# Balancing the sort matrices with row products written transposed

## The chip, the cores and the metric

The kernel runs on one core of a Trainium2 chip. Its engines work side by side, each on its own queue of instructions: TensorE (PE) multiplies matrices, VectorE (DVE) and ScalarE (ACT) do elementwise work and reductions, GpSimd (POOL) does small elementwise work and issues most loads, SyncE (SP) issues transfers. They wait for each other by semaphores. The metric is the device time of one execution in microseconds (us).

## The reference

There are 32 sort matrices of 8 x 8 (4 batches of 8 heads). Each is balanced in five rounds; then its rows mix the eight blocks of keys and values, block attention follows, and a feed-forward network with two first layers takes the larger of both. What the change touches is the first loop:

```
P = sort_net                                   # (4, 8, 8, 8)
for _ in range(5):
    P = P - np.max(P, axis=-1, keepdims=True)
    P = np.exp(P)
    P = P / (np.sum(P, axis=-1, keepdims=True) + 1e-09)
    P = P / (np.sum(P, axis=-2, keepdims=True) + 1e-09)
k_sorted = np.einsum('bhij,bhjcd->bhicd', P, k_b)
v_sorted = np.einsum('bhij,bhjcd->bhicd', P, v_b)
...
```

The rest is softmax(q k_sorted^T / 8) v_sorted for each of the eight blocks of 96 tokens, and then max(x w1, x w2) w_out on 3072 tokens of width 512. Sequence 768, head width 64, inner width 1024.

## The kernel before, in words

The kernel is one list of steps, written out by hand as short tokens (the string `plan`), which the function `token` turns into instructions one after the other. Each engine runs its own instructions in that order. So the list alone sets what stands in front of what on an engine, and nothing is reordered later. The start of the list, which holds the five rounds of balancing (S0 to S4), the masks (m0 to m3), the first turns of v (tv) and the block diagonal matrices made of the result (D0, B0), reads:

```
lw1 lw2 I1 lk0.0 lk0.1 lk0.2 lq0.0 lq0.1 lq0.2 S0 m0 S1 m1 S2 m2 tv0.18A S3 tv18.36A lq0.3
J1 S4 m3 tv36.56A tv56.80A D0 g1 tv80.96D g2 g3 a2.0.1 B0 k0.1A k0.0A k0.2A b0.0A q0.0D
```

**Balancing** (`sinkhorn`, lines 269 to 288). The tile p_sb holds one matrix on each of 32 partitions, 64 floats in the order i, j (row, column). A round has one ScalarE instruction, the exponential (L270), and six on VectorE: the row sums (L276), their reciprocals (L277), the product of each row with its own (L278), the column sums (L281), which read p_sb with i and j exchanged, that is 8 floats or 32 bytes apart from number to number, their reciprocals (L282), and the product of each column with its own (L283). The last product of the fifth round goes to p_bf in bf16. The subtraction of the maximum is left out, since it cancels. In the fourth and fifth round (`it >= 3`) a tile of zeros is set (L88) and TensorE is given filler matmuls (L83, tile fill_ps), which compute nothing that is used.

**Beside it.** TensorE runs fillers from the start. ScalarE copies pieces of v (L250, `turn_v`), reading pairs of bf16 numbers 128 bytes apart and writing in order; VectorE copies one such piece as 4-byte words (L255). VectorE also makes the masks (L294 to L311) behind the rounds, and POOL the selections (L211, L218, L226) and more masks (L1068) once its first loads are issued.

**Behind it.** `block_diagonals_first` multiplies p_bf on TensorE (L361, L368), VectorE makes the block diagonal matrix for the keys (L376), and TensorE mixes the keys with it (L489, tile k_ps). ScalarE copies that out of PSUM (L109, tile kT), and scores (L584), exponentials (L599), values (L612), their division by the sums (L629) and the feed-forward layers (L805, L961) follow. Queries are turned in PSUM and copied out to the tile qT, by L109 in order for batch 0 and by L466 with pairs of bf16 numbers written 192 bytes apart for batch 1. The masked sums L391 and L342 are two reductions of VectorE that read in order, of 64 and of 320 floats a partition. Batches 1 to 3 have transposes of x by DMA (tile xT).

Of the kernel before, what the change touches and what calls it, by code (L numbers as in the profile page):

```python
# [10 lines left out]
FP32 = mybir.dt.float32  # L11
# [5 lines left out]
def kernel(  # L17
# [16 lines left out]
    nc = tc.nc  # L34
    AF = mybir.ActivationFunctionType
    ALU = mybir.AluOpType
    AX = mybir.AxisListType

    B, H, S, D = q.shape
    NB = sort_net.shape[-1]  # L40
    BLK = S // NB
    G = B * H
# [13 lines left out]
    const = ctx.enter_context(tc.tile_pool(name="const", bufs=1))  # L56
# [10 lines left out]
    def ps_f32(name):  # L67
        return psum.tile([128, 1024], FP32, tag="ps", name=name)
# [9 lines left out]
    def keep_streaming(ps, n, by=None, most=512):  # L78

        w0 = fill[:, 0:128] if by is None else late[by]  # L80
        while n > 0:
            w = min(n, most)
            nc.tensor.matmul(ps[:, 0:w], w0, fill[:, 0:w], start=True, stop=True)  # L83
            n -= w

    def late_zeros(by):
        late[by] = const.tile([128, 128], BF16, tag=f"late{by}", name="late")
        nc.vector.memset(late[by], 0.0)  # L88
# [25 lines left out]
    p_sb = const.tile([G, NB, NB], FP32, tag="p_sb", name="p_sb")  # L114
# [150 lines left out]
    rowsum = const.tile([G, NB], FP32, tag="rowsum", name="rowsum")  # L265
    colsum = const.tile([G, NB], FP32, tag="colsum", name="colsum")
    p_bf = const.tile([G, NB, NB], BF16, tag="p_bf", name="p_bf")

    def sinkhorn(it, meanwhile=None):
        nc.scalar.activation(out=p_sb, in_=p_sb, func=AF.Exp)  # L270
        if meanwhile:
            meanwhile()
        if it >= 3:
            late_zeros(it)
            keep_streaming(ps_f32("fill_ps"), 3072, it)
        nc.vector.reduce_sum(out=rowsum, in_=p_sb, axis=AX.X)  # L276
        nc.vector.reciprocal(out=rowsum, in_=rowsum)  # L277
        nc.vector.tensor_tensor(  # L278
            out=p_sb, in0=p_sb, in1=rowsum.to_broadcast([G, NB, NB]), op=ALU.mult
        )  # L280
        nc.vector.reduce_sum(out=colsum, in_=p_sb.transpose([0, 2, 1]), axis=AX.X)  # L281
        nc.vector.reciprocal(out=colsum, in_=colsum)  # L282
        nc.vector.tensor_tensor(  # L283
            out=p_bf if it == 4 else p_sb,
            in0=p_sb,
            in1=colsum.to_broadcast([G, NB, NB]).transpose([0, 2, 1]),
            op=ALU.mult,
        )

# [791 lines left out]
    def token(text):  # L1081
# [8 lines left out]
        elif kind == "J":  # L1090
            first_selections()
        elif kind == "S":
            sinkhorn(n[0])
        elif kind == "m":
            masks(n[0]) if n[0] < 3 else spread_masks()
# [141 lines left out]
```

## Time and profile before

| | |
|---|---|
| median of the runs shown | 156.07 us (155.84 to 156.44) |
| the profiled execution | 156.11 us |
| its span, first to last instruction | 154.3 us |
| busy: PE, DVE, ACT, POOL | 147.4, 134.7, 102.0, 25.3 us |
| first exponential starts, p_bf is written | 2.49 us, 11.49 to 11.70 us |
| first matmul of the attention (L361) | 11.76 us |
| granted clock of TensorE | 1.00 in the mean |

The profile is a record of one execution. Its chain of waits goes back from the last instruction to what released it, and on to the first; shares and times of that chain tell what set the end. A group has the line of the code, the engine, the operation, the written tile, an arrow, the read tiles, the shape, and how many there were; behind the bar stand busy us and mean ns of one; behind the next bar the idle time ahead of them. Busy shares alone mislead here: PE is busy in the first 12 us, but with fillers.

### The profile page before, as it was taken

Reading aid. Unit: us, or ns where it says so; the run is one execution under the profiler, and the core shown is the slowest. Engines: PE = TensorE matmul, PEld = TensorE weight load, DVE = VectorE, ACT = ScalarE, POOL = GpSimd, SP = SyncE. Lnnn points to the kernel's source line nnn. Section 1 sums busy time; section 2 is a strip of 40 time slices with the busy share of each in tenths; the row PEclk is TensorE's granted clock in tenths of the full one; section 3 lists DMA queues with packets and bytes.
Section 4 is the critical chain, followed back from the end, with each engine's and each line's share of the span. In section 5 each row is a group of like instructions: output and inputs, shape, how many; then the busy total and the mean of one; then the engine's idle time right before and its main releaser. Section 6 shows DMA issues by size and latency. Waiting matters only on the chain.

```text
span 154.3 us, 5157 instructions
## 1 busy us (share of the span) xinstructions
PE 147.4 (96%) x2238; PEld 114.0 (74%) x2238; DVE 134.7 (87%) x287; ACT 102.0 (66%) x134; POOL 25.3 (16%) x53
## 2 busy tenths in 40 slices
PE   6999989999999999999999999989999999999991
PEld 6948867555678788887567998765688978578881
DVE  4888989999999999986999999658899999999731
ACT  3488897268899997879859797888792301463010
POOL 7999541100210400001500000000000000000000
PEclk9999999999999999999999999999999999999999
DMA  3999999999999972998999939996001475500065
GB/s 45 197 207 197 197 204 207 217 215 215 216 215 199 205 155 57 150 133 219 287 205 211 188 62 150 165 195 253 0 4 24 85 116 203 187 6 0 0 224 184
DMA packets 28918, 23.93 MB, mean 155 GB/s; under 512 B 16672, under 2 KB 24608, under 8 KB 28896
## 3 DMA queue, kind: packets, MB, share of 16 engines
q0 software_dynamic: 9280, 13.37, 49.1%
q1 hardware_dynamic: 19200, 9.84, 28.9%
q10 hardware_dynamic: 416, 0.39, 0.8%
q8 instruction: 17, 0.28, 0.7%
q14 instruction: 5, 0.04, 0.1%
HBM read 26.75 MB, written 6.29 MB: 214 GB/s over the span
## 4 chain that ended last, share of the span: by engine, by line
PE 62%; DVE 24%; ACT 4%; DMA 3%; issue 3%; DVEq 0%
PE out_ps L961 32%; PE hb_ps L805 10%; PE hq_ps L805 8%; PE o_ps L612 4%; DVE g L824 4%; DVE x L629 3%; PE k_ps L489 3%; PE s_ps L584 3%; DMA xT<-x 2%; ACT kT L109 2%; DVE w_sb L771 2%; PE v_ps L554 1%; DVE v_dc L255 1%; DVE sums_x L891 1%; DVE w_sb L236 1%
## 5 line engine op out<-in xcount | busy, mean ns | idle before, releaser
L805 PEld LDWEIGHTS <-w_sb 128*128 128x128 bf16 x224 | 21.5, 98 | 14.7 <-issue 0.8
L599 ACT ACTIVATE e<-s_ps 96x768 bf16<-96x768 f32 x32 | 24.1, 807 | 2.2 <-PE s_ps L584 2.0
L629 DVE TENSOR_TENSOR x<-o_ps,rs 96x512 bf16<-96x512 f32 x32 | 22.0, 686 | 1.1
L996 ACT COPY o<-out_ps 128x512 f32<-128x512 f32 (+1 forms) x18 | 8.6, 479 | 21.5 <-PE out_ps L961 21.2
L961 PEld LDWEIGHTS <-g 128*128 128x128 bf16 x192 | 18.2, 98 | 2.4
L805 PE MATMUL hb_ps<-sums_x,w_sb 128*128 128x384 bf16 x96 | 18.2, 327 | 0.0
L961 PEld LDWEIGHTS <-sums_g 128*128 128x128 bf16 x144 | 13.5, 97 | 2.2 <-issue 0.2
L961 PE MATMUL out_ps<-wo_sb,g 128*128 128x256 bf16 x96 | 13.1, 273 | 0.0
L987 DVE TENSOR_TENSOR o<-out_ps,o 128x512 f32<-128x512 f32 (+1 forms) x16 | 8.9, 553 | 4.7 <-PE out_ps L961 4.6
L109 ACT CAST kT<-k_ps 128x1024 bf16<-128x1024 f32 x12 | 11.6, 1020 | 2.0 <-PE k_ps L489 2.0
L805 PE MATMUL hq_ps<-xT,w_sb 128*128 128x384 bf16 x64 | 12.7, 326 | 0.0
L612 PE MATMUL o_ps<-v_sb,e 96*128 96x65 bf16 x256 | 12.4, 194 | 0.0
L612 PEld LDWEIGHTS <-e 96*128 96x128 bf16 x256 | 10.7, 98 | 1.5 <-DVE x L629 0.2
L961 PE MATMUL out_ps<-w2T,sums_x 128*128 128x256 bf16 x72 | 11.8, 273 | 0.0
L584 PE MATMUL s_ps<-qT,kT 64*128 64x96 bf16 x256 | 9.2, 204 | 1.1 <-ACT qT L109 0.7
L111 DVE CAST v_sb<-v_ps 96x1024 bf16<-96x1024 f32 x8 | 9.6, 1214 | 0.2 <-PE v_ps L531 0.2
L961 PEld LDWEIGHTS <-sums_x 128*128 128x128 bf16 x96 | 8.6, 97 | 1.2
L584 PEld LDWEIGHTS <-kT 64*128 64x128 bf16 x256 | 6.4, 94 | 3.5 <-issue 2.6
L826 ACT ACTIVATE g<-g 128x768 bf16<-128x768 bf16 x7 | 5.9, 842 | 4.4 <-DVE g L824 4.4
L83 PE MATMUL fill_ps<-fill 128*128 128x118 bf16 x92 | 7.3, 264 | 1.2 <-DVE fill L74 1.2
L176 POOL DMA_DIRECT2D v_raw<-in_v_dram x11 | 6.5, 597 | 11.2 <-DVE v_dc L255 4.3
L109 ACT CAST v_sb<-v_ps 96x1024 bf16<-96x1024 f32 x8 | 7.8, 1016 | 0.6 <-PE v_ps L554 0.6
(129 smaller groups left out, 304.2 us busy)
## 6 DMA issues: line engine op xcount, KB each, us to landing
out_dram<-o SPq DMA_DIRECT2D x10, 512.0 KB, 2.9
v_raw<-in_v_dram POOLq DMA_DIRECT2D x8, 384.0 KB, 16.2
k_raw<-in_k_dram POOLq DMA_DIRECT2D x3, 768.0 KB, 10.8
w_sb<-in_moe_w_dram POOLq DMA_DIRECT2D x4, 256.0 KB, 7.6
wo_sb<-in_moe_w_out_dram POOLq DMA_DIRECT2D x2, 512.0 KB, 11.2
w_sb<-in_moe_w_dram POOLq DMA_DIRECT2D x2, 512.0 KB, 14.8
v_raw<-in_v_dram POOLq DMA_DIRECT2D x3, 256.0 KB, 4.7
k_raw<-in_k_dram POOLq DMA_DIRECT2D x3, 256.0 KB, 6.4
```

The lines of the kernel that those rows point to most:

```text
L83: nc.tensor.matmul(ps[:, 0:w], w0, fill[:, 0:w], start=True, stop=True)
L109: nc.scalar.copy(out=out_ap, in_=in_ap)
L111: nc.vector.tensor_copy(out=out_ap, in_=in_ap)
L176: nc.gpsimd.dma_start(out=v_raw[r0 : r0 + 64, m * n : (m + 1) * n], in_=v_src[b, :, m * n : (m + 1) * n],)
L584: nc.tensor.matmul(ps[:, h2 * 512 + ii * 128 : h2 * 512 + ii * 128 + BLK], kT[b][rows, (hp * 8 + i) * BLK : (hp * 8 + i) * BLK + 128], rhs ...
L599: nc.scalar.activation(out=e_out, in_=src, func=AF.Exp, scale=scale)
L612: nc.tensor.matmul(ps[:, h2 * 512 + ii * 65 : h2 * 512 + (ii + 1) * 65], e[:, (h2 * 4 + ii) * BLK : (h2 * 4 + ii) * BLK + 128], v_sb[:, m0 ...
L629: nc.vector.tensor_tensor(out=x, in0=ov[:, :, :, 0:D], in1=rs.to_broadcast([BLK, 2, 4, D]), op=ALU.mult,)
L805: nc.tensor.matmul(ps[:, m * 512 : m * 512 + TCH], w[:, k, c : c + 128], x[:, k], start=new and k == 0, stop=k == 1, skip_group_check=True,)
L961: ins = nc.tensor.matmul(self.ps[:, bank * 512 + p * NW : bank * 512 + (p + 1) * NW], left(self.b, lw, k, ti * 128), right(rw, k), start=n ...
L987: ins = nc.vector.tensor_tensor(out=self.part(ch, half), in0=self.by_tile(self.bank(n)), in1=other, op=ALU.add)
L996: ins = nc.scalar.copy(out=out, in_=self.by_tile(self.bank(n)))
```

## The change

A new tile p_t, 32 partitions of 64 floats, holds the matrices in the order j, i. The row product reads p_sb as before and writes p_t, in the order i, j of the instruction, so that each number is written 32 bytes behind the last. The column sums read p_t in order. The column product reads and writes p_t in order, with each column's factor repeated along the inner axis; in the fifth round it reads p_t in order and writes p_bf across, numbers of 2 bytes 16 bytes apart, so that p_bf holds what it held before. From the second round on the exponential reads p_t across, 32 bytes from float to float, and writes p_sb in order; the first round's works in p_sb as before. The list of steps, the number of instructions and their order on every engine are the same.

```diff
+    p_t = const.tile([G, NB, NB], FP32, tag="p_t", name="p_t")
 
     def sinkhorn(it, meanwhile=None):
-        nc.scalar.activation(out=p_sb, in_=p_sb, func=AF.Exp)
+        if it:
+            nc.scalar.activation(out=p_sb, in_=p_t.transpose([0, 2, 1]), func=AF.Exp)
+        else:
+            nc.scalar.activation(out=p_sb, in_=p_sb, func=AF.Exp)
...
         nc.vector.tensor_tensor(
-            out=p_sb, in0=p_sb, in1=rowsum.to_broadcast([G, NB, NB]), op=ALU.mult
-        )
-        nc.vector.reduce_sum(out=colsum, in_=p_sb.transpose([0, 2, 1]), axis=AX.X)
+            out=p_t.transpose([0, 2, 1]),
+            in0=p_sb,
+            in1=rowsum.to_broadcast([G, NB, NB]),
+            op=ALU.mult,
+        )
+        nc.vector.reduce_sum(out=colsum, in_=p_t, axis=AX.X)
         nc.vector.reciprocal(out=colsum, in_=colsum)
         nc.vector.tensor_tensor(
-            out=p_bf if it == 4 else p_sb,
-            in0=p_sb,
-            in1=colsum.to_broadcast([G, NB, NB]).transpose([0, 2, 1]),
+            out=p_bf.transpose([0, 2, 1]) if it == 4 else p_t,
+            in0=p_t,
+            in1=colsum.to_broadcast([G, NB, NB]),
             op=ALU.mult,
         )
```

## The prediction

> **What bounds the kernel now.** I read the page's chain of waits first, then the same chain in order of time, then the instructions that write or read the tile p_sb, then the groups kept apart by shape.
>
> ```profile
> PE 62%; DVE 24%; ACT 4%; DMA 3%; issue 3%; DVEq 0%
> ```
>
> Over the whole span TensorE is the bound, but the change lies in the first 12 us, and there the chain is another. The chain in order of time, with start, length, engine and tile (one iteration, and the handover to the sorting of the keys):
>
> ```profile
> 6.41 0.22 DVE rowsum L276
> 6.65 0.20 DVE rowsum L277
> 6.88 0.22 DVE p_sb L278
> 7.13 0.27 DVE colsum L281
> 7.42 0.20 DVE colsum L282
> 7.65 0.22 DVE p_sb L283
> 7.89 0.26 ACT p_sb L270
> 8.18 0.22 DVE rowsum L276
> ...
> 11.49 0.22 DVE p_bf L283
> 11.76 0.36 PE pe L361 x8
> 12.19 0.23 DVE bd L376
> 12.47 0.71 PE k_ps L489 x32
> 13.20 2.84 ACT kT L109 x3
> ```
>
> Six VectorE instructions and one exponential follow each other with 0.02 to 0.04 us between them, five times, and the end of the last releases the first useful matmul (L361). So every instruction of the balancing is on the path, and a nanosecond added to one of them is added to the start of the attention. The PE work beside it (fill_ps) is filler that computes nothing, so it hides nothing.
>
> The tile's own rows, with the shortest, median and longest time in ns:
>
> ```profile
> L270 ACT ACTIVATE p_sb<-p_sb x5: 255/255/257, 2.5 to 9.8; 32x64 f32<-32x64 f32 x5
> L276 DVE TENSOR_REDUCE rowsum<-p_sb x5: 206/207/207, 2.8 to 10.1; 32x8 f32<-32x64 f32 x5
> L278 DVE TENSOR_TENSOR p_sb<-p_sb,rowsum x5: 213/267/390, 3.2 to 10.6; 32x64 f32<-32x64 f32 x5
> L281 DVE TENSOR_REDUCE colsum<-p_sb x5: 254/259/260, 3.6 to 11.0; 32x8 f32<-32x64 f32 x5
> L283 DVE TENSOR_TENSOR p_sb<-p_sb,colsum x4: 211/211/301, 4.1 to 9.5; 32x64 f32<-32x64 f32 x4
> ```
>
> L276 and L281 are the same reduction of the same 64 numbers. L276 reads them in order, L281 reads them 8 floats (32 bytes) apart, and takes 257 ns on average instead of 207. This 50 ns is what reading across costs, and the only thing that the change can win.
>
> **The change part by part.** No instruction is added or removed, and no engine's order changes; both programs issue the same list. Tiles and patterns change. Four terms, all on the path.
>
> 1. *The column sums read in order.* Five times 257 becomes 207: 5 x 0.050 = **-0.25 us**. This is certain within a few ns, because L276 is the same operation.
>
> 2. *The row products write across.* Five multiplies of 64 floats (now L278) write each float 32 bytes behind the last. In the fifth iteration the last multiply (L283) writes p_bf across as well, with bf16 numbers 16 bytes apart. That makes six such writes. The trace of before has no VectorE write of single elements at such a distance, so the cost is bounded. Lower end: nothing, if only reads suffer. (Below nothing is excluded: reads and arithmetic are as before.) For the other end I use these groups, with mean ns behind the bar:
>
> ```profile
> L391 DVE TENSOR_REDUCE pt<-pm 128x8 f32<-128x64 f32 x1 | 0.2, 220 | 0.0
> L342 DVE TENSOR_REDUCE pt<-pm 128x40 f32<-128x320 f32 x1 | 0.5, 486 | 0.0
> L109 ACT COPY qT<-tq_ps 128x1536 bf16<-128x1536 bf16 x1 | 1.4, 1439 | 0.0
> L466 ACT COPY qT<-tq_ps 128x1536 bf16<-128x1536 bf16 x2 | 3.0, 1548 | 0.0
> ```
>
> The first two give VectorE's rate in order: (486 - 220) / 256 = 1.04 ns an element. L281 is 50 / 64 = 0.78 ns worse, so a read that finds one element in each place costs 1.82 ns. The last two are the same ScalarE copy of 1536 numbers out of PSUM; L109 writes in order, L466 writes pairs 192 bytes apart. A pair costs 2 x 0.82 ns in order (0.82 from (1439 - 1020) / 512, with 1020 for the 1024 elements of kT) and (1548 - 1439) / 768 = 0.14 more apart: 1.78 ns a place. Reads and writes thus agree on some 1.8 ns for a visit to a new place. With it a VectorE write across costs 64 x (1.8 - 1.04) = 49 ns, and six cost **+0.29 us**. I take this end and not zero, because its row is a write, and because the read of the very same tile says the same.
>
> The Trainium skill, "SBUF — State Buffer", section "Door 1: The DMA port swizzle", says that SBUF is accessed in 16-byte lines and needs at least two hits a line for full bandwidth, without setting reads apart from writes. By that rule all six writes pay, and the sum would be the one that I take; L281 against L276 shows it for reads only, and no row of before shows it for a VectorE write.
>
> 3. *The exponential reads across.* Four of the five (iterations 1 to 4; the first still reads p_sb in order). No ScalarE row reads single elements apart. Lower end: nothing; L250 reads pairs 128 bytes apart, at (1519 - 1189) / 384 = 0.86 ns an element against 0.82 in order. But a pair in 1.72 ns is also just what one place in 1.8 ns allows. One float in each place would then cost 1.8 instead of 0.82, so 64 x 0.98 = 63 ns. I take this: **+0.25 us** for four. In each iteration the next row sum starts 0.02 to 0.03 us after the exponential ends, so nothing covers it; the masks that VectorE does meanwhile end at the same moment.
>
> 4. *The rest.* The second multiply now takes colsum repeated along the inner axis, which L278 did with rowsum: 211 to 213 ns either way where nothing disturbs, so nothing. The exponential waits in addition for an earlier ScalarE instruction, which its own queue ended long before: nothing, as everything queued behind it (the v copies of L250) had 0.4 to 0.6 us of idle time in front of the next exponential. POOL's last mask tile (sel_k) is ready at 10.87, its reader starts at 12.06: cover on both sides. The zeros for the late filler (L88) are behind L283 and move along. No queue of DMAs waits for the balancing.
>
> Sum: -0.25 + 0.29 + 0.25 = **+0.29 us** at the start of the key sorting. From there it goes through: ScalarE's three kT copies follow L489 back to back, VectorE is busy 31.38 of 32.40 us from 20.0 to 52.4, PE 46.39 of 46.40 from there to 98.8, the 3.65 us landing of xT is counted from its issue, and PE makes up nearly all of the rest. The profiled execution took 156.11 us, span 154.3 and 1.81 around it, so I forecast 156.11 + 0.29 = **156.4 us**. The median of the runs shown, 156.07, is 0.04 below the profiled execution; by it the sum would be 156.36. This is +0.2%. A measurement of this kernel can tell about 0.5%, 0.78 us, from no change.
>
> **The rivals.**
>
> *Writes are free, the exponential pays* (156.1). -0.25 + 0.25 = 0. [...] Against it: L466. If of the two only the exponential were free, the sum would be +0.04, 156.15; that is the same time.
>
> *No pattern costs anything but the reduction* (155.9). -0.25. For it: L255, a VectorE copy that reads 4-byte words 128 bytes apart at (830 - 599) / 256 = 0.90 ns a word, less than the 1.04 of a read in order. Against it: L255 has one source and is another operation, and L281's 50 ns need a reason that is not its pattern. The Trainium skill, "VectorE: DVE Perf Modes", section "Mode 1× (REGULAR) — the baseline", states one result a cycle with any stride, which gives this result; L281 goes against it, and no row shows a write. The same page's section "Mode 2×_2P — use both read ports for one tensor" would explain L255 as two streams, each at half its rate.
>
> *The loss is swallowed* (156.1). At 19.62 the chain has 0.58 us of "issue", idle time before a score matmul (20.20) that no row explains. If that matmul waits for something that does not move with the balancing, 0.29 fits into it. Against it: VectorE is busy without a break from 16.04 to 20.56, and PE's earlier work shifts.
>
> *The writes fetch before they write* (157.1, slower). If a write of four bytes into a line takes two visits, fetch and put, each of the six costs 64 x (2 x 1.8 - 1.04) = 164 ns, 0.98 in all, and the sum is -0.25 + 0.98 + 0.25 = +0.98. It comes out over 0.78 from 131 ns a write on. Where POOL works beside it, L278 already went from 213 to 390 ns. Against it: L466, where a pair takes one visit's time, not two.
>
> *Events elsewhere* decide for 0.8 us or more, either way: the new tile p_t is 256 bytes a partition and moves every tile behind it in SBUF, and the packets of the loads meet the engines at other moments. Nothing in the profile shows that either matters; the instruction lists are the same.
>
> **How the numbers follow.** Forecast 0.48; writes free 0.15; swallowed 0.10; no pattern costs 0.08; fetch before write 0.09; events elsewhere 0.10 (0.04 faster, 0.06 slower). The range takes the forecast with both ends of its unknown costs (155.86 if all are nothing) and reaches up to the fetching writes, 157.1; below I leave 0.26 us more, about the distance of the lowest of the runs shown (155.84) from the profiled one: **155.6 to 157.1**. Within 0.5% are the forecast and the first three rivals, 0.81, and a third of the fetching writes, for prices under 131 ns: same 0.84. Slower by more: 0.06 + 0.06 = 0.12. Faster by more: 0.04.
>
> **What would show it.** In the profile of the changed kernel: colsum's reduction at 207 ns (step 1); the row multiply at about 260 where POOL is idle, and the last one the same (step 2); the exponential at 255 the first time and 318 four times (step 3); the first L361 matmul at 12.05 instead of 11.76. If the multiplies stay at 213, the first rival is right; if the exponentials stay at 255 too, the second; at 340 or more, the fetching writes. If 12.05 is reached and the span still is 154.3, the loss was swallowed. What would make the prediction wrong is a cost for one visit that differs from 1.8 ns on the write side, since six of the ten changed instructions that can lose are writes.

## The result, and the profile after

The changed kernel takes 156.66 us (median of 11 runs, 156.26 to 157.61), the kernel before in the same measurement 156.04 (11 runs): 0.62 us more by the medians, ratio 1.0051, interval 1.0029 to 1.0072. A ratio leaves out executions that were over 1.5% above the fastest of their kernel, so it need not be the quotient of the medians. A second measurement on another chip gave 156.55, ratio 1.0025 [0.9995, 1.0056], an interval that just includes no change. So there is most likely a small loss, 0.4 to 0.8 us by the middles of the two. The forecast was 156.4.

The profiled execution took 157.61 us, span 155.7. It is the slowest of the 11, so its end says too much; its first 22 us are what is read here above all. The instructions that read or write the new tile p_t, shortest, median and longest in ns:

```profile
L282 DVE TENSOR_TENSOR p_t<-p_sb,rowsum x5: 264/266/303, 3.2 to 10.9; 32x64 f32<-32x64 f32 x5
L288 DVE TENSOR_REDUCE colsum<-p_t x5: 207/207/207, 3.5 to 11.2; 32x8 f32<-32x64 f32 x5
L290 DVE TENSOR_TENSOR p_t<-p_t,colsum x4: 211/212/319, 4.0 to 9.7; 32x64 f32<-32x64 f32 x4
L272 ACT ACTIVATE p_sb<-p_t x4: 315/317/318, 4.3 to 10.1; 32x64 f32<-32x64 f32 x4
L290 DVE TENSOR_TENSOR p_bf<-p_t,colsum x1: 431/431/431, 11.7 to 11.7; 32x64 bf16<-32x64 f32 x1
```

Steps 1 to 3 can be read off. The column sums fell from 257 to 207. The row products rose from 211 to 214, where nothing stretched them, to 264 to 268. The exponentials rose from 255 to 315 to 318. One row is far from its forecast: the product that writes p_bf takes 431 ns, where 260 was forecast.

The chain of waits of the changed kernel in order of time (start, length, engine, tile) shows two more things, at the exponential and at 20 us. The two lines behind it are the chain of the kernel before at 20 us:

```profile
7.74 0.22 DVE p_t L290
7.97 0.02 issue
7.99 0.02 ACTq L272
8.01 0.04 issue
8.05 0.33 ACT p_sb L272
...
11.66 0.44 DVE p_bf L290
12.10 0.04 issue
12.15 0.36 PE pe L368 x8
...
18.57 1.43 ACT qT L109
20.00 0.71 ACT e L606
20.71 0.45 issue
21.16 0.35 PE s_ps L591 x8
```

```profile
19.62 0.58 issue
20.20 0.35 PE s_ps L584 x8
```

Before, the exponential began 0.02 us behind the product (7.87 to 7.89). Now there is a piece "ACTq" between them, an instruction of ScalarE's queue, and 0.08 us pass. The first useful matmul (L361, now L368) starts at 12.15 and not at 11.76. And the score matmul at 20.20 starts at 21.16: the 0.39 us have become 0.96. PE now waits 1.16 us behind the end of the copy to qT, 0.58 before. From there the first out_ps matmul is 0.96 later too (46.75 to 47.71), the keys of batch 2 1.60 (82.34 to 83.94, where this execution waits for the load of k_raw), and the last matmul 1.40. So 0.64 us of this profile's loss come in at 82 us, at another wait.

### The profile page after: what moved, and what is told of

Same layout as the page of the kernel before. It is cut to its first block, busy times and chain, and to the rows that moved or that the text cites. A ratio compares the mean times of both kernels' runs of the same rounds, so it can differ in the third digit from the quotient of the medians.

```text
span 155.7 us, 5158 instructions
## 1 busy us (share of the span) xinstructions
PE 146.2 (94%) x2235; PEld 113.1 (73%) x2238; DVE 135.1 (87%) x287; ACT 102.4 (66%) x134; POOL 25.5 (16%) x53
## 4 chain that ended last, share of the span: by engine, by line
PE 53%; DVE 24%; DMA 12%; ACT 5%; issue 3%; POOL 0%; POOLq 0%; DVEq 0%; ACTq 0%
PE out_ps L968 31%; PE hb_ps L812 7%; DMA k_raw<-in_k_dram 6%; PE hq_ps L812 5%; DMA xT<-x 5%; PE o_ps L619 4%; DVE g L831 3%; DVE x L636 3%; PE k_ps L496 3%; DVE v_dc L255 2%; ACT kT L109 2%; PE s_ps L591 2%; DVE w_sb L778 1%; PE v_ps L561 1%; DVE sums_x L898 1%
## 5 line engine op out<-in xcount | busy, mean ns | idle before, releaser
L250 ACT COPY v_dc<-v_raw 64x1152 bf16<-64x1152 bf16 (+3 forms) x6 | 8.2, 1379 | 0.0
```

The source lines that it names most:

```text
L250: nc.scalar.copy(out=dst.rearrange("p (d c two) -> p d c two", c=BLK, two=2)[:, :, c0:c1], in_=src.rearrange("p (c d two) -> p d c two", c ...
```

## The experiments

Two questions: where the loss in the balancing comes from, and what becomes of it at 20 us. My theory for the second formed while reading the two traces. The page has a DMA queue for instructions:

```profile
q8 instruction: 17, 0.28, 0.7%
```

Its 17 packets have 16384 bytes each. PE has some 4490 instructions (each matmul is two, a weight load and the product), so about 256 a packet. Counting PE's instructions in the program, the matmul at 20.20 is number 706. The unexplained stops of PE in the kernels below stand at numbers 450, 706 and 1474, which are 256 k - 62; in the kernel before only the one at 706 is seen. The trace's packets show a regular course: PE passes such a number, a transfer of the instruction queue starts (3.4 to 4.1 us later at 14 us, while POOL's loads fill the DMA engines, within 0.3 us at 93, 100 and 114 us, where those loads have ended; the last transfer starts 1.3 us ahead of its number, so PE's passing is not all that sets it), and PE passes the next such number no sooner than 2.2 to 2.5 us after that start. So the theory says that PE waits at 20 us for its own instructions, and that their transfer stands among the loads.

### Prices of patterns

Instructions are added behind the last step, each twice; nothing else changes.

```diff
+    mul(apart(raw, 8, 512), a, b2)      # 64 products, fp32 written 32 bytes apart
+    mul(apart(half, 8, 1024), a, b2)    # the same, bf16 written 16 bytes apart
+    total(apart(raw, 8, 0).rearrange("p (m n) -> p m n", n=8))
+    exp(raw[:, 2700:2764], apart(raw, 8, 0))
...
```

> The kernel before, with a row of extra instructions at its end on data that nothing uses, each twice: products, sums and exponentials of 64 numbers on 32 partitions, with one operand 4, 8, 16 or 32 bytes apart. The end is later by some 10 us and is not compared. Theory: fp32 writes 8 bytes apart cost nothing (213), 16 and 32 bytes apart 264; fp32 pairs 32 bytes apart 213; bf16 in order 213, single bf16 numbers apart cost 430, already at 4 bytes if the part of a 4-byte word is what costs, only from 16 bytes on if the place is; bf16 pairs 213 if the word is what costs. Sums 207 at 4 and 8 bytes, 257 at 16 and 32. Exponentials 255 at 4 and 8 bytes, 317 at 16 and 32; written 32 bytes apart 317 in fp32, and more in bf16 if ScalarE has the same cost for parts of a word. Rival: what the last product of the changed kernel lost (431) was the meeting with POOL's loads; then single bf16 numbers apart take 264 here, where POOL is idle.

Two of the products in the view by line, in narrow windows, fp32 written 32 bytes apart and bf16 written 16 bytes apart:

```profile
L1223 DVE TENSOR_TENSOR v_raw<-v_raw x1: 261/261/261, 156.2 to 156.2; 32x64 f32<-32x64 f32 x1
L1223 DVE TENSOR_TENSOR v_raw<-v_raw x1: 428/428/428, 158.9 to 158.9; 32x64 bf16<-32x64 f32 x1
```

The rival fell: 428 ns at a time at which POOL does nothing. Read in the same way, for 64 numbers on 32 partitions, in ns (ScalarE's rows ran beside VectorE's):

| | in order | 4 B apart | 8 B | 16 B | 32 B | pairs 16 or 32 B apart |
|---|---|---|---|---|---|---|
| VectorE product, fp32 written | 212 to 214 | | 213 to 215 | 259, 260 | 261 | 212, 214 |
| the same, bf16 written | 212, 214 | 220 | 287, 290 | 428 | | 212, 216 |
| VectorE product, one operand read | 212 to 214 | | | | 246, 253 | |
| VectorE sum, read | 197, 207 | | 207, 208 | 252, 254 | 253, 254 | |
| ScalarE exponential, read, fp32 written | 255 | | 257 | 312, 315 | 314 | |
| the same, read in order, fp32 written apart | 255 | | | | 315, 317 | |
| the same, read in order, bf16 written apart | | | | 484, 485 | | |

Sixty-four fp32 numbers, each alone in its 16 bytes, cost VectorE 45 to 49 ns more when written, about 46 more when read by a sum and 32 to 41 more when read as one operand of a product; they cost ScalarE 57 to 62 more. At 8 bytes' distance, two to each 16, the distance costs nothing. The Trainium skill, "SBUF — State Buffer", section "Door 1: The DMA port swizzle", gives lines of 16 bytes of which two hits are needed. The fp32 rows agree with it. The bf16 rows do not: at 8 bytes' distance two numbers fall in each line, and the write still costs 75 ns more. A bf16 number written 16 bytes from the last is 3.4 ns dearer than in order (216 / 64), a single float 0.7 (47 / 64); bf16 as pairs, so 4 bytes together, and floats as pairs cost nothing. The price of single bf16 numbers rises with the distance, 220, 288, 428 ns, so neither of my two theories for it (already at 4 bytes, only from 16 on) holds; why it rises stays open.

### The second wait, and the last round

In the first kernel each round's exponential of the changed kernel writes a tile of its own, so that nothing has to wait for ScalarE's own earlier write:

```diff
-            nc.scalar.activation(out=p_sb, in_=p_t.transpose([0, 2, 1]), func=AF.Exp)
+            p_own = const.tile([G, NB, NB], FP32, tag=f"p_own{it}", name="p_own")
+            nc.scalar.activation(out=p_own, in_=p_t.transpose([0, 2, 1]), func=AF.Exp)
```

> The changed kernel, but each round's exponential writes a tile of its own (four more tiles of 64 floats) instead of p_sb, so that it waits for VectorE alone and not for an earlier ScalarE instruction as well. In the changed kernel each of the four exponentials of rounds 2 to 5 starts 0.09 to 0.10 us after the VectorE product ends, in the kernel before 0.03 to 0.04. Theory: the second wait is an instruction of its own in ScalarE's queue and costs 0.06 us each time. Then the gap goes back to 0.04 and the first matmul of the attention (12.15 in the changed kernel) starts at about 11.9. Rival: the gap comes from reading a tile across (the first float is later), then it stays 0.10 and the matmul stays at 12.15.

In the second the fifth round of the changed kernel is that of the kernel before:

```diff
+        if it == 4:
+            nc.vector.tensor_tensor(
+                out=p_sb, in0=p_sb, in1=rowsum.to_broadcast([G, NB, NB]), op=ALU.mult
+            )
+            nc.vector.reduce_sum(out=colsum, in_=p_sb.transpose([0, 2, 1]), axis=AX.X)
...
```

> The changed kernel, but the fifth round works as before: row product in p_sb in order, column sums read across, last product to p_bf in order. Theory: writing numbers of 2 bytes 16 bytes apart is what made the last product take 431 ns instead of 213; the visits of 16-byte places that I reckoned with (264) are not enough for it. Then the last product takes 213, the fifth column sum 257, the fifth row product 213 where POOL leaves it alone, and the first matmul starts at about 11.93 instead of 12.15. Rival: the last product is slowed by the loads that POOL issues at the same time (from 10.86 on); then it stays above 400.

The first took 156.6 us, ratio 1.0034 [1.0002, 1.0066]; the second 156.36, 1.0009 [0.9977, 1.0041]. The intervals overlap each other and that of the change, so the whole times settle little; the rows do. Both first matmuls came at 12.05 and not at 11.9, as expected, since these executions began their first exponential 0.17 and 0.09 us later; so the times from there are compared. With own tiles, the chain in order of time:

```profile
7.79 0.22 DVE p_t L292
8.01 0.02 issue
8.03 0.32 ACT p_own L273
```

The piece of ScalarE's queue is gone and 0.02 us pass again: the second wait cost 0.06 us a round, 0.24 in four. The rival, that reading across is what delays the start, fell, since this kernel reads across as well. From the first exponential to the first useful matmul pass 9.43 us instead of 9.71. With the fifth round as before, its products take 213 and 214 ns and its column sum 257; 9.52 us pass. So the write of p_bf across is what took 431 ns, and not the loads of POOL, which are issued here at the same time. (The profile of that kernel has a granted clock of 0.989, all of it lost behind 22 us; its end is not used.)

### Pairs: the same change without single numbers

From the first row product on the matrices are kept as (h, j, l), with rows 2h and 2h+1 side by side, in the kernel before. Every access then finds two floats together, and each exponential works in its tile.

```diff
+    pp = const.tile([G, NB // 2, NB, 2], FP32, tag="pp", name="pp")
...
+        nc.vector.reduce_sum(out=colsum, in_=pp.transpose([0, 2, 1, 3]), axis=AX.XY)
```

> The kernel before with another layout: from the first row product on, p lies as (row pair, column, row in the pair), so that both sums and all products find two neighbours of 4 bytes in each place of 16 bytes: row sums read floats 8 bytes apart, column sums read pairs 64 bytes apart. p_bf is written in order. No exponential waits twice. Theory (it is single elements, one in each place of 16 bytes, that cost 0.8 ns more, and pairs cost nothing): all reductions take 207, all products 211 to 213 where POOL leaves them alone, the first matmul starts at 11.5 and the kernel is 0.25 us faster than before, ratio 0.998. Rival (any departure from the order costs, or a pattern of three dimensions does): the column sums stay at 257 or the row sums rise to it as well, and the time is that of before or up to 0.3 us more.

It took 156.1 us, ratio 1.0015 [0.9988, 1.0043]. The rows of the tile pp:

```profile
L297 DVE TENSOR_REDUCE colsum<-pp x5: 206/207/210, 3.3 to 10.2; 32x8 f32<-32x64 f32 x5
L274 ACT ACTIVATE pp<-pp x4: 255/256/256, 4.0 to 9.2; 32x64 f32<-32x64 f32 x4
L287 DVE TENSOR_TENSOR pp<-pp,rowsum x4: 211/212/257, 4.8 to 9.9; 32x64 f32<-32x64 f32 x4
```

All that the change was charged for is gone, and the 50 ns of each column sum are won. The first useful matmul starts at 11.05, 0.71 us earlier than in the profile of before. And the score matmul at 20 us starts at 20.25, 1.21 us behind the end of the copy to qT: the gain of this execution ends there, and the expected ratio of 0.998 was missed.

### Delays

Zeros are set in a tile of their own on VectorE ahead of the last product of the kernel before, two times 218 ns in one kernel, four times in the other. No pattern and no wait of the balancing changes.

```diff
+        if it == 4:
+            nc.vector.memset(idle, 0.0)
+            nc.vector.memset(idle, 0.0)
```

> The kernel before, with two memsets of 192 floats on VectorE between the last reciprocal and the last product; they set a tile that nothing reads, and nothing else is changed. They are to delay p_bf by about 0.39 us, as the change did. Theory: what the change costs behind the balancing is the same delay handed on; then the first matmul starts at 12.15, and the end is later by 0.39, or by as much more as the score matmul that follows the query copy at 20.2 us loses (0.58 us of idle time before it in the profile of before, 1.16 after): ratio 1.0025 to 1.005. Rival: the end moved because p_t shifts all later tiles in SBUF, not because of the delay; but this kernel's tile shifts them too, so a kernel with an unused p_t alone is to follow. If the delay is swallowed the ratio is 1.000.

> The kernel before, with four memsets of 192 floats on VectorE before the last product instead of two (the kernel with two started its first matmul at 11.62, since its products happened to meet nothing of POOL's, and ended at 1.0011 of before). The delay is about 0.85 us against before. Theory (instruction transfer): a request that comes after about 14.7 us gets behind one more load and is served 1.0 to 1.2 us later (18.9 instead of 17.7 to 18.0); the score matmul goes from 20.2 to about 21.2 and the time is up by 0.8 to 1.1 us, ratio 1.005 to 1.007, as much as or more than the changed kernel's. Rival (nothing but the delay counts): the matmul is later by 0.85 less the 0.58 of idle time, and the time is up by 0.27, ratio 1.0017.

With two, 156.18 us, ratio 1.0011 [0.9986, 1.0036]; with four, 157.15, 1.0076 [1.005, 1.0102], with the score matmul at 21.01, 0.96 us behind the copy to qT. The first expectation was missed: its kernel's first matmul came at 11.62 and not at 12.15, since none of its products was stretched, and nothing measurable was lost. Four sets of zeros, a delay somewhat larger than the change's, lose as much as the change or more. So a delay alone is enough for such a loss; that the changed kernel's loss has no other part does not follow. A kernel with an unused p_t alone was not run. The tile of zeros moves the tiles behind it too, and with two sets of zeros that cost nothing measurable.

### Another place of the boundary

The first filler of PE is cut into fewer matmuls for the same columns. Each one less takes two instructions from PE's program, so that number 706 falls on a later step. Two kernels have 46 instead of 92, without and with the pairs; then 84 and 80 with the pairs, and 84 alone.

```diff
-    keep_streaming(ps_f32("fill_ps"), 92 * 118, most=118)
+    keep_streaming(ps_f32("fill_ps"), 92 * 118, most=236)
```

> The kernel before, with the first filler of TensorE issued as 46 matmuls of 236 columns instead of 92 of 118: the same columns streamed, 92 instructions fewer on PE's queue (a matmul is two). Theory: the idle time of 0.58 us before the score matmul at 20.2 is PE waiting for its own instructions. They come in transfers of 16 KB, 17 of them for 4491 instructions, so some 256 a transfer; each starts when PE passes a multiple of 256, and under the loads it stands 3 to 4 us in the DMA queues; the matmul at 20.2 is instruction 706 of the program, which is 3 x 256 less what runs ahead of it. With 92 instructions fewer the score matmul starts 0.05 us after the query copy (L109) ends, the idle time goes or stands some 90 instructions later (in the scores at 22 to 23 us), and the time is 0 to 0.6 us less than before, ratio 0.996 to 1.000. Rival (the matmul waits for a landing of w2 or for something on ScalarE): the idle time stays before the same matmul, at 20.2.

> The pair layout (both neighbours in each place of 16 bytes) together with the wider filler. In the pair layout alone the first matmul started at 11.05 instead of 11.76, but the score matmul at 20.25 as before, behind 1.21 us of idle time. Theory (instruction transfer): with the boundary moved, the score matmul starts right after the query copy, at about 19.1, and the kernel is 0.4 to 0.9 us faster than before, ratio 0.994 to 0.9975, unless the transfer of the next block stops it some 90 instructions later; then it is that of f1. Rival: it stays at 20.2 and the time at that of before.

Both expectations of a gain failed: 163.54 us, ratio 1.0372 [1.0313, 1.043], and 163.68, 1.0453 [1.0397, 1.0508]. The wait left number 706's old place, but it came at an earlier block and not some 90 instructions later, as I had expected. The timeline of PE with 46 fillers alone has it at number 450:

```profile
14.92 0.58 PE L510 MATMUL v_ps<-bd,v_dc 64*128 64x64 bf16 x14
17.79 0.62 PE L510 MATMUL v_ps<-bd,v_dc 64*128 64x64 bf16 x16 [2.29 <-issue]
```

With 92 instructions fewer, number 194 lies behind the fillers, so that the transfer with number 450 was asked for at 12.26 and not at 8.94, started at 15.45, and PE went on at 17.79, 2.34 us behind the start. A second stop follows at number 1474, 2.51 us up to 52.22, again 2.44 us behind the start of a transfer (49.78). Behind each of the two the granted clock is lower, 0.50 from 20 to 26 us and from 54 to 56:

```profile
PEclk9999857999999599999999999999999999999999
```

So most of the loss of these kernels is two stops and the slow stretches behind them. The last round as before, with one stop of 1.57 us ahead of 21.48, has a granted clock of 0.50 from 23 to 25 us, with the short fillers. Stops of up to 1.2 us (the change, four delays) are not followed by such a stretch. That a stop lowers the clock is argued from this order in time; it was not tried by itself.

> The kernel before, with the balanced matrices kept as pairs from the first row product on (p as h, j, l, two rows beside each other), and the first filler of PE cut into 84 matmuls of about 130 columns in place of 92 of 118: the same streamed columns, 16 instructions of PE fewer. Theory (PE waits for its own instructions, whose next block of 256 is asked for at a fixed place of the program and begins 62 instructions ahead of a multiple of 256): the boundary that held the first score matmul of the seventh tile of scores (20.20 in before, 20.25 with the pairs alone) moves 16 instructions further on, behind that score matmul. So the score matmul follows the copy of qT at once (about 19.1), and the wait is found at a values matmul, at about 20.2 and shorter for the work that now stands ahead of it. First useful matmul at 11.0 as with the pairs alone (8.74 us behind the first exponential); the gain of 0.3 to 0.6 us then reaches the end in part: 155.5 to 155.8, ratio 0.996 to 0.999. Rival (the idle time at 20.2 belongs to that score matmul, for a reason of its own, such as its operand): it stays in front of the score matmul at 20.2, ratio 1.000 to 1.002 as with the pairs alone.

> As the kernel with 84 filler matmuls, but with 80 of about 136 columns, 24 instructions fewer than before. Theory: the boundary moves 24 instructions on, so the idle time of PE is found 24 instructions behind the place that it had, and the next block is asked for later by the 8 instructions more: the ratio is that of the 84 within 0.002, unless the earlier boundary (in front of the sorting of the keys) begins to hold PE as well, as it did with 46 fillers (1.037). Rival: the idle time stays in front of the same score matmul.

> The kernel before, with the first filler alone cut into 84 matmuls of about 130 columns; the balancing is untouched. Theory: the boundary moves 16 instructions on, the idle time in front of the seventh tile's score matmul (0.58 us) goes and comes back at a values matmul a little later. With the same late block, most of it comes back: ratio 0.998 to 1.001. Rival: the idle time stays where it was; ratio 1.000.

| | median us | ratio |
|---|---|---|
| pairs, 84 fillers | 157.1 | 1.0056 [1.0024, 1.0087] |
| pairs, 80 fillers | 158.37 | 1.0126 [1.0074, 1.0178] |
| 84 fillers alone | 156.64 | 1.0031 [1.0, 1.0062] |

The place moved as the theory said, in all three; the gain did not come. The timeline of PE of the kernel with pairs and 84 fillers, where number 706 is the first values matmul (L634):

```profile
19.03 0.35 PE L606 MATMUL s_ps<-qT,kT 64*128 64x96 bf16 x8 [0.21 <-ACT qT L109]
20.43 0.40 PE L634 MATMUL o_ps<-v_sb,e 96*128 96x65 bf16 x8 [1.06 <-DVE w2T L111]
```

The score matmul now starts 0.05 us behind the copy of qT, so its operand or its tile was never what it waited for. The next stop is 0.50 us behind the end of the copy (w2T, 19.25 to 19.93) that its row names. Number 706 is passed at 20.4, and all VectorE work behind it hangs on this matmul instead: its first division starts at 20.87 against 20.93 in before. The block of instructions, not the place of its boundary, is late. With 84 fillers alone the matmul starts 0.08 us behind that copy, so there the copy may hold it as well. With 80 fillers number 450 stops PE for 1.11 us at 14.37, as with 46, and number 706 stops it once more. The kernel with pairs and 84 fillers ends 0.85 us later than before in its profile, though it starts the division earlier: 0.3 of it come in at 82 us, at a load of keys, the rest at 103.35, where PE waits 1.22 us for a load of xT (0.56 in before). Why those loads land later stays open.

### The changed kernel again

> The changed kernel once more, for a second profile on another chip. Theory: exponentials 255 and four of 315 to 318 ns, products of the rows 264 to 268 except where POOL is met, p_bf about 430, 0.09 to 0.10 us from the end of a column product to the next exponential; the first useful matmul 9.5 to 9.7 us behind the first exponential, the wait ahead of the seventh tile's score matmul about 1.1 us, it starts at 21.0 to 21.3; ratio 1.003 to 1.007. Rival (the wide wait at 20 us was luck of that one profile): the score matmul starts at 20.5 to 20.6, with 0.58 us ahead of it.

The second profile: 264 to 266 ns for four row products, 315 to 317 for the exponentials, 432 for p_bf, 9.71 us from the first exponential to the first matmul, just as in the first. But the wait at 20 us is that of the rival; its chain in order of time:

```profile
19.87 0.56 issue
20.44 0.35 PE s_ps L591 x8
```

Here my expectation was wrong, and the instruction queue tells why. From the trace's packets and the count of PE's instructions, in us of the span:

| | first useful matmul | number 450 passed | transfer starts | number 706 passed |
|---|---|---|---|---|
| pairs | 11.05 | 13.87 | 17.82 | 20.25 |
| pairs, 84 fillers | 11.12 | 14.04 | 18.03 | 20.44 |
| 84 fillers alone | 11.25 | 14.16 | 17.75 | 20.13 |
| two delays | 11.62 | 14.21 | 17.61 | 19.93 |
| before | 11.76 | 14.35 | 17.70 | 20.20 |
| the change, second profile | 12.01 | 14.61 | 17.97 | 20.44 |
| own tiles | 12.05 | 14.64 | 17.99 | 20.19 |
| last round as before | 12.05 | 14.79 | 19.03 | 21.48 |
| four delays | 12.20 | 14.81 | 18.55 | 21.01 |
| the change, first profile | 12.15 | 14.83 | 18.94 | 21.16 |

For requests from 13.87 to 14.64 the transfer starts between 17.6 and 18.0, however early they are. From 14.79 on it starts between 18.5 and 19.0. In every row number 706 is passed 2.2 to 2.5 us behind the start of the transfer, though the starts lie up to 1.4 us apart; that is the strongest sign that the transfer sets it. A shift of 0.2 us across that edge costs some 0.7 us at once, and a gain on the near side gives nothing at this place. The changed kernel stands at the edge: two executions of it fell on different sides.

What is lost or won at 20 us is not yet what is lost at the end. The start of one and the same instruction of PE, against the profile of before, in us later:

| | at 23 us | at 80 us | at 83 us | at 110 us |
|---|---|---|---|---|
| pairs | 0.05 | 0.04 | 0.19 | 0.42 |
| two delays | -0.27 | 0.07 | 0.23 | -0.07 |
| own tiles | -0.01 | -0.02 | 0.82 | 0.78 |
| the change, second profile | 0.24 | 0.25 | 0.36 | 0.42 |
| four delays | 0.81 | 0.80 | 0.80 | 0.37 |
| the change, first profile | 0.96 | 0.97 | 1.66 | 1.42 |

From 23 to 80 us the difference stays in most rows. Then PE meets two loads: k_raw of batch 2 at 82 us, and a transposed load of xT at 99 to 103 us. Own tiles lose nothing at 20 us and all of their 0.78 us at the first of them:

```profile
83.09 1.71 PE L498 MATMUL k_ps<-bd,k_raw 64*64 64x64 bf16 x96 [0.76 <-DMA k_raw<-in_k_dram]
```

These two places move single profiles by -0.4 to +0.8 us, as much as the whole effect, and what sets their landings was not tried.

## Why the prediction was near the time, and wrong on the way

The time, 156.66 against 156.4, lies in the range, and its rise of 0.4 to 0.5% is at the bound that I set between "same" and "slower". The way there was partly luck. Of the steps:

**Step 1, the column sums**, 257 to 207: as forecast, -0.25 us.

**Step 2, the writes across.** The five fp32 writes cost 52 ns each (266 against 214) where 49 were forecast; the estimate from a visit to a new place held, and the rivals of free writes and of fetching writes fell. The sixth, p_bf, was mis-sized: I gave it the price of a float, +49 ns. It cost +218 (431 against 213), and the measured prices above show why: single 2-byte writes are a case of their own. My two sources for the price of a place were a read of floats and a write of bf16 pairs; neither is a single 2-byte write.

**Step 3, the exponentials**: +62 ns each, 63 forecast, +0.25 us in four.

**Step 4 failed**, and with it "No instruction is added or removed": "The exponential waits in addition for an earlier ScalarE instruction, which its own queue ended long before: nothing". That the thing waited for is long done does not make the wait free. ScalarE got an instruction of 17 ns in its queue in each of the four rounds, and 0.06 us more pass each time, 0.24 in four. The Trainium skill, "Perfetto Trace Analysis", section "Identifying Dependency Chains", notes that instructions which wait for several engines may get such an instruction ahead of them; the trace agrees (here the two engines are VectorE and ScalarE itself), and the kernel with own tiles shows the price.

The sum in the balancing is thus -0.25 + 0.26 + 0.22 + 0.25 + 0.24 = +0.72 us, and not +0.29. It was not seen at its full size since the profile of before is an unlucky one. From the first exponential to the first useful matmul it has 9.27 us, of which 0.44 are four products of up to 390 ns. The profiles of the four kernels that have the same balancing (two and four delays, 46 and 84 fillers alone) have no such product; that with 84 fillers:

```profile
L278 DVE TENSOR_TENSOR p_sb<-p_sb,rowsum x5: 211/211/214, 3.2 to 10.2; 32x64 f32<-32x64 f32 x5
```

It passes 8.83 us. The changed kernel has 9.71, of which 0.15 are stretched products, so 9.56: +0.73, which the sum explains.

**"From there it goes through"** failed too. I had named the idle 0.58 us at 19.62 as a rival, "the loss is swallowed", and dropped it since everything around was busy. A loss is neither swallowed there nor handed through as it is. PE waits there for a block of its instructions, whose transfer starts in the loads' time and not in the balancing's. Nor does it go through at 82 and at 99 to 103 us, where the landings of k_raw and xT add or take up to 0.8 us; there the rival "events elsewhere", of which I had said that nothing shows that it matters, was nearer to what the runs show. The table of shifts, each against the 8.83 us of undisturbed balancing, with the ratio of the whole:

| | first exponential to first useful matmul | shift | ratio |
|---|---|---|---|
| pairs | 8.74 | -0.09 | 1.0015 [0.9988, 1.0043] |
| two delays | 9.18 | +0.35 | 1.0011 [0.9986, 1.0036] |
| own tiles | 9.43 | +0.60 | 1.0034 [1.0002, 1.0066] |
| last round as before | 9.52 | +0.69 | 1.0009 [0.9977, 1.0041] |
| the change | 9.71 | +0.88 | 1.0051 [1.0029, 1.0072], 1.0025 [0.9995, 1.0056] |
| four delays | 9.85 | +1.02 | 1.0076 [1.005, 1.0102] |

The first 0.35 us cost nothing that can be measured, and the last two rows cost 0.4 to 1.2 us. The last round as before does not fit: it shows no loss, though its profile lies beyond the edge; so the shift alone does not set the ratio. The forecast of +0.29 was near the end by luck: a loss in the balancing more than twice as large, part of it not seen at the end. That the wait at 20 us is one for instructions is shown by where it moved with the count of fillers, and by its fixed distance from the transfer. That POOL's loads are what holds the transfer back is argued only and was not tried. What speaks for it: where packets of their queue (q0) ran in the 2 us ahead, the lag was mostly 2.6 to 4.2 us, though at times under 1, and at most 1.4 where the packets of the transposes (q1) filled the engines as well or none ran.

## What to carry to other kernels

Price a transposed access by what stands together: here 8 bytes of floats together, or pairs of bf16, cost nothing, a single float in its 16 bytes 0.5 to 1 ns more, and a single bf16 number written 16 bytes from the last 3.4 to 3.6 ns more. Count the engines that an instruction waits for, not only when they are done: a second one cost 0.06 us here. Before a gain is claimed at the end, look for the first idle time that no row explains and ask what sets it; here the transfer of PE's own instructions started at a time of its own, so that gains vanished at that place and losses beyond an edge grew. Then look at which later loads PE nearly waits for: they can change the sign of the rest.

## What the runs showed that I had not expected

- PE's instruction blocks are not hidden in this kernel: 0.4 to 2.4 us of idle PE ahead of number 450 or 706, and 2.5 and 3.1 ahead of number 1474 with 46 fillers. The Trainium skill, "Runtime: NRT & Kernel Launch", section "Instruction fetch mechanics", has blocks of 16 KiB or 256 instructions, which the 17 packets of 16384 bytes agree with, and their cost as mostly hidden, which 20 us here does not bear out.
- Single bf16 numbers written 16 bytes apart: 428 ns against 212 on VectorE, 484 on ScalarE, where floats in order take 255.
- The same products took 211 to 390 ns in one execution and 211 to 214 in another. The long ones lie beside instructions of POOL (the one of 390 beside its copy to sel_k at 10.59), but one beside such an instruction took 211 (at 3.2, with 84 fillers alone). What decides it was not tried.
- Stops of PE of 1.57, 2.29 and 2.51 us at instruction blocks were followed by 2 to 6 us at a granted clock of 0.50. One of 1.93 us, for xT with 80 fillers, was not followed by slower work, so the length of the stop alone does not decide.
